# Seven products in the fourth column group of a chunked-attention and feed-forward kernel

## The chip, the cores and the metric

The kernel runs on one core of one Trainium2 chip. The metric is the device time of one execution in microseconds; the kernel before is given by the median of three executions. One further execution was profiled, and every row below comes from that one.

## The reference

The inputs are q, k and v of shape (8, 8, 576, 64) in float32 (batch, heads, sequence, head dimension) and two weight matrices. Attention looks only within chunks of 64 positions:

```python
scores = scale * np.matmul(q_c, k_c.transpose(0, 1, 2, 4, 3))
scores = scores - np.max(scores, axis=-1, keepdims=True)
attn = np.exp(scores)
attn = attn / (np.sum(attn, axis=-1, keepdims=True) + 1e-09)
out = np.matmul(attn, v_c)
...
h = x @ w_in            # x: 4608 x 512, w_in: 512 x 2048
g = h - np.tanh(h)
return g @ w_out        # w_out: 2048 x 512
```

## The kernel before, in words

The 4608 tokens are 36 pairs of 64-token chunks, in nine groups of four pairs (512 tokens). Groups 0 and 1 go through `FeedForward`; groups 2 to 8 go through `Fast`, each as two halves of 256 tokens (b = 0, 1). A half is done in eight **units**, one for each column group j = 0 to 7; column group j is the pair of 128-column blocks j and j + 8 of `w_in`. So a group takes 16 units; unit number s counts from 0 at group 2, and group 4 begins at s = 32. While one group runs, the attention of the next one is prepared between its units.

**A unit** has a first product (x times `w_in`, into the PSUM tile `ph`), the nonlinearity (ScalarE's tanh at line 725, VectorE's `shrink` at line 732, three GpSimd additions at lines 733 to 735), a split into two float16 parts (`gh` on ScalarE, line 744, and `gl` on VectorE, line 745) and a second product (`gemm2`, line 764), which is itself done with seven products. Each float16 product is three terms, high by high, low by high and high by low. The stages of one unit are spread over four units of TensorE's order: in unit s the kernel issues the first product of s, the tanh and shrink of s - 1, the split of s - 2 and the second product of s - 3. `ph` has two buffers.

**The first product has two forms.** In `gemm1` (line 691) it is 24 matmuls of 256 columns. From group 4 on (`SEVEN = 4`, blocked operands) it can also be seven block products (`Fast.seven`, matmuls on line 706), 42 matmuls of 128 columns. These need sums of weight blocks, made once for each j, and sums of x blocks, made once for each half. The seven products come in two parts. Four of them (P5, P4, P1, P6; 24 matmuls) are issued first. Then `kept_back` (ScalarE, line 711) copies three quarters of `ph` to SBUF and `joined` (VectorE, lines 715 and 716) adds two of them up in `ph`. After `gemm2` the other three products (P2, P7, P3; 18 matmuls) accumulate on what `joined` wrote, so they wait for it. One unit later `completed` (VectorE, line 721) does the last additions, ahead of the tanh of that unit. `in_seven` (line 955) decides which units take this form: in the kernel before all from group 4 on, but not j = 3, not j = 0 to 3 of group 4's first half, and not j = 6, 7 of group 8's second half. That is 65 of the 80 units.

**The order of issue** is written out: each engine runs its instructions in program order. `run` (line 812) calls the stages of a unit, and at two places in each unit it calls what stands in the list `at`: `at[o + 2 * s]` after the first product, ahead of tanh, `kept_back` and `joined`; `at[o + 2 * s + 1]` at the unit's end. `beside` (line 958) and `ahead` (line 998) put the attention's steps of group g into those lists by unit and part, the functions of one place in the order of `put`. For the groups from 5 on, in units counted within the running group and alike for both halves (u = 3 and u = 11): `scores` in unit 4 (12), part 1; `largest`, `shifted`, `exponent`, `totals`, `divided`, `high`, `transpose` (two transposing DMAs on SyncE), the split of v, then `values` (96 small matmuls) in part 0 and `blocks` in part 1 of units 11 and 19, that is of j = 3 of either half. `blocks` (line 416) issues, twice, a ScalarE multiply to float16 (line 425), a ScalarE multiply to float32 (line 426) and a VectorE subtraction (line 427). `halves` (line 304, VectorE, line 311) is in part 0 of the unit after, j = 4. `finish` (line 768; five VectorE additions at line 777) follows the second product of j = 7, which is issued in the unit j = 2 of the next half.

`spread` (line 283) puts a broadcast of the greatest |v| by two TensorE matmuls (line 290) into a corner of a PSUM bank of the second product, and `greatest` (line 292, VectorE, line 296) reads it; the second product can't write that bank before. It needs both `halves`. For group 4, `spread` and `greatest` stand in unit 8 of group 3's run.

**The weight-block sums** (`Half.seven`, line 535): a generator of seven steps for each j, six GpSimd operations (lines 539 to 548), two ScalarE copies (lines 560 and 564), two VectorE subtractions (line 556) and, but for j = 7, two DMAs into DRAM (`kept`). `make_in` (line 1243) runs the steps in the lists; before, there are seven such j (none for j = 3), one every 7.25 half-units, beginning 22 half-units before group 3 and ending 28 half-units into it. In the blocked stage the sums of j = 0 to 5 are loaded again from `kept` for each half, two units ahead, into one of three buffers (`load`, line 841).

In the opening, written as the string `PLAN`, a token F*n* issues n matmuls of 512 columns on a zero tile (`warm`, line 1102), which compute nothing that is used.

Of the kernel before, what the change touches and what calls it, by code (L numbers as in the profile page):

```python
# [23 lines left out]
H = 8  # L24
# [7 lines left out]
FC = DFF // P  # L32
# [23 lines left out]
l0.0 A0 A1 l1.0 v0 v1 a2 a3 l0.1 v2 v3 l1.1 l2.0 l2.1 a4 a5 l3.0 l3.1 F15 x0.0 b0.0 i0.0 z0.0 W0.0 S0 S1 q0 x1.0 m0 p0 e1 P1 F13 S2 N0 T0 b1.0 i1.0 S3 N1 x0.1 z1.0 W1.0 T1 F2 m2 p2 e3 U2 V0 F3 G0.0 D2 P3.0 P3.1 b0.1 U3 D3 i0.1 t T2 x1.1 b1.1 G1.0 t T3 s i1.1 z0.1 W0.1 F2 V2 s z1.1 W1.1 H Y G0.1 x2 G1.1 b2 t s i2 t x3 z2.0 w2.0 s z2.1 w2.1 H h S4 S5 b3 i3 | l4.0 l4.1 v4 v5 z3.0 w3.0 z3.1 w3.1 M4 g2 h l5.0 l5.1 c4 M5 g3 h N4 N5 T4 T5 V4 a6 a7 l6.0 l6.1 c5 S6 S7 v6 v7 g4 h E6 l7.0 l7.1 c6 g5 h M7 l8.0 l8.1 c7 g6 h n6 N7 g7 h T6 T7 V6 Z c8 l9.0 l9.1 c9 g8 h l10.0 l10.1 c10 g9 h l11.0 l11.1 c11 g10 h X l12.0 l12.1 c12 g11 h l13.0 l13.1 c13 g12 h l14.0 l14.1 c14 g13 h l15.0 l15.1 c15 g14 h  # L56
# [3 lines left out]
def attn_ffn_kernel(ctx: ExitStack, tc: tile.TileContext, qE, kE, vE, qL, kL, vL, w_in, w_out, out):  # L60
# [894 lines left out]
    def in_seven(g, b, j):  # L955
        return j != 3 and (g, b, j // 4) != (SEVEN, 0, 0) and (g, b, j // 6) != (NG - 1, 1, 1)

    def beside(att, at, g):
# [7 lines left out]
        late = 2 * (g == SEVEN)  # L966
        put(4 + late, 0, att.halves, g, 1)
        put(6 + late, 0, att.spread, g)
        put(6 + late, 1, att.greatest, g)
        put(12, 1, lambda: powers.update({g: half.power_of(g)}))  # L970
        for b, u in enumerate((3, 11)):
# [9 lines left out]
            put(u + 6, 1, att.split_high, g, b)  # L981
            put(u + 7, 0, att.split_low, g, b)
# [8 lines left out]
            if g + 1 < NG:  # L991
                for i in range(2):
                    p = FIRST[g + 1] + 2 * b + i, 2 * b + i
                    put(u + 2 + i, 1, att.load, *p, "q")
                    put(u + 4 + i, 1, att.load, *p, "k")
                    put(u + 7, 1, att.load, *p, "v")

    def ahead(att, at, g):
# [17 lines left out]
        for b, u in enumerate((3, 13) if late else (6, 14)):  # L1016
# [5 lines left out]
            u += late - before * (1 + b)  # L1022
            for i in (2 * b, 2 * b + 1):
                put(u + 2, 1, att.load, FIRST[g + 1] + i, i, "qk")
            put(u + 2, 0, att.scores, g, b)
# [217 lines left out]
    def make_in(i, j):  # L1243
        if j not in made_in:
            made_in[j] = half.seven(j, temporary[i % 2] if i else stream[2], stream[i % 2] if j < FC // 2 - 1 else temporary[1], j == FC // 2 - 1)
# [5 lines left out]
    steps = [[29 * i // 4 - 22 + k for k in (0, 1, 2, 4, 5, 6, 7)] for i in range(FC // 2 - 1)]  # L1251
# [86 lines left out]
```

## Time and profile before

| | |
|---|---|
| median of three executions | 788.44 us (787.76 to 788.88) |
| the profiled execution, its own time | 788.26 us |
| its span, first to last instruction | 786.5 us |
| TensorE busy | 769.9 us, 98% of the span, 9832 matmuls |
| VectorE busy | 635.7 us, 81% |
| ScalarE busy | 480.0 us, 61% |
| GpSimd busy | 501.9 us, 64% |
| mean granted TensorE clock | 0.998 |
| HBM traffic over the span | 105 GB/s |

The profiled execution is 0.18 us below the median; 1.8 us of it lie outside the span. Busy time of TensorE is modelled and overlaps between neighbours, so the share alone doesn't say that TensorE is the bound; the gaps between its instructions do. In the rows PE is TensorE, PEld its weight loads, DVE VectorE, ACT ScalarE, POOL GpSimd and SP SyncE.

### The profile page before, as it was taken

The page shows a single profiled execution, that of the slowest core. Times are in us where ns is not written, and L with a number is a line of the kernel's source. Part 1 is how long each engine was busy: PE and PEld are TensorE (multiplying, and loading weights), DVE is VectorE, ACT ScalarE, POOL GpSimd, SP SyncE. Part 2 cuts the span into 40 slices and gives each one's busy share as a digit, 9 for nine tenths or more (in the row PEclk, how much of TensorE's full clock was granted, in tenths as well). Part 3 has the DMA queues.
Part 4 walks back from the last instruction along what each step waited for, and adds up shares of the span by engine and source line. Part 5 has one row for each costly group of instructions (what it writes and reads, how often), then busy time and mean ns, then how long its engine had stood idle before and what let it go on. Part 6 is the DMA issues. An engine that isn't in the chain of part 4 may idle for free. (4 is left out here: it accounts for less than half of the span.)

```text
span 786.5 us, 23238 instructions
## 1 busy us (share of the span) xinstructions
PE 769.9 (98%) x9832; PEld 663.8 (84%) x9835; DVE 635.7 (81%) x1021; ACT 480.0 (61%) x787; POOL 501.9 (64%) x572
## 2 busy tenths in 40 slices
PE   7999999999999999989999999999999999999997
PEld 4878886666788878878899998999899989999996
DVE  5896998788698888697878887888888878797565
ACT  5877988556466454454656574747565656566443
POOL 1100001587678888789677778677867786868763
PEclk9999999999999999999999999999999999999999
DMA  9865441210232323133262635354544442424110
GB/s 349 289 201 181 162 161 53 78 31 1 82 81 95 82 83 103 49 94 122 65 230 60 202 67 176 96 173 98 156 113 139 127 144 57 135 56 135 55 55 28
DMA packets 74600, 91.68 MB, mean 117 GB/s; under 512 B 34560, under 2 KB 41728, under 8 KB 74496
## 3 DMA queue, kind: packets, MB, share of 16 engines
q1 hardware_dynamic: 74064, 89.55, 36.9%
q8 instruction: 77, 1.26, 0.7%
q10 hardware_dynamic: 432, 0.66, 0.3%
q14 instruction: 27, 0.22, 0.1%
HBM read 70.25 MB, written 12.58 MB: 105 GB/s over the span
## 5 line engine op out<-in xcount | busy, mean ns | idle before, releaser
L733 POOL TENSOR_TENSOR xl<-xl 128x256 f32<-128x256 f32 x111 | 146.5, 1320 | 114.7 <-DVE xl L732 103.2
L725 ACT ACTIVATE t<-ph,sig 128x512 f32<-128x512 f32 x112 | 77.0, 687 | 152.6 <-DVE ph L721 123.2
L691 PE MATMUL ph<-xh,wh 128*128 128x256 f16 x1068 | 123.7, 273 | 0.2 <-DVE xl L732 0.2
L691 PEld LDWEIGHTS <-wh 128*128 128x128 f16 x1068 | 103.5, 98 | 12.9 <-issue 0.9
L732 DVE SCALAR_TENSOR_TENSOR xl<-ph,sig,t 128x512 f32<-128x512 f32 x112 | 83.2, 743 | 28.8 <-ACT t L725 28.6
L706 PE MATMUL ph<-xh,wl 128*128 128x128 f16 x1344 | 97.8, 219 | 0.0
L764 PEld LDWEIGHTS <-gh 128*128 128x128 f16 x924 | 88.1, 98 | 10.1 <-issue 0.4
L706 PE MATMUL ph<-xh,wh 128*128 128x128 f16 x1332 | 95.7, 219 | 0.9 <-DVE ph L716 0.8
L764 PEld LDWEIGHTS <-wl 128*128 128x128 f16 x882 | 85.2, 98 | 12.2 <-issue 2.6
L745 DVE SCALAR_TENSOR_TENSOR gl<-xl,to_g,gh 128x896 f16<-128x896 f32 x68 | 84.8, 1246 | 8.8 <-ACT gh L744 8.8
L764 PE MATMUL po<-wl,gh 128*128 128x256 f16 x610 | 87.9, 273 | 0.2 <-DVE wl L777 0.2
L706 PEld LDWEIGHTS <-wh 128*128 128x128 f16 x1332 | 81.7, 98 | 4.8 <-DVE ph L716 3.6
L764 PE MATMUL po<-wl,wl 128*128 128x256 f16 x549 | 82.1, 273 | 2.5 <-DVE most L296 2.5
L735 POOL TENSOR_TENSOR xl<-xl 128x256 f32<-128x256 f32 x111 | 82.7, 745 | 0.0
L706 PEld LDWEIGHTS <-wl 128*128 128x128 f16 x1344 | 81.0, 98 | 0.8
L744 ACT ACTIVATE gh<-xl,to_g 128x896 f16<-128x896 f32 x68 | 71.0, 1044 | 15.1 <-POOL xl L735 14.8
L734 POOL TENSOR_TENSOR xl<-xl 128x128 f32<-128x128 f32 x111 | 69.4, 625 | 0.0
L745 DVE SCALAR_TENSOR_TENSOR wl<-xl,to_g,wl 128x896 f16<-128x896 f32 x44 | 56.1, 1274 | 4.6 <-ACT wl L744 4.6
L605 PE MATMUL ph<-xh,wh 128*128 128x512 f16 (+2 forms) x252 | 59.7, 380 | 0.0
L764 PE MATMUL po<-wh,wl 128*128 128x256 f16 x333 | 59.7, 273 | 0.0
L744 ACT ACTIVATE wl<-xl,to_g 128x896 f16<-128x896 f32 x44 | 45.9, 1043 | 15.7 <-POOL xl L735 14.6
L636 PE MATMUL po<-wh,gh 128*128 128x512 f32 x128 | 52.8, 415 | 0.0
(231 smaller groups left out, 1599.2 us busy)
## 6 DMA issues: line engine op xcount, KB each, us to landing
wl<-kept SPq DMA_DIRECT2D x96, 256.0 KB, 3.8
raw<-w_in SPq DMA_DIRECT2D x16, 512.0 KB, 3.7
raw<-w_out SPq DMA_DIRECT2D x16, 512.0 KB, 4.8
xl<-qL SPq DMA_DIRECT2D x28, 256.0 KB, 3.9
rawv<-vL SPq DMA_DIRECT2D x28, 256.0 KB, 3.0
rawk<-kL SPq DMA_DIRECT2D x28, 256.0 KB, 4.5
out<-wl SPq DMA_DIRECT2D x55, 128.0 KB, 2.4
kept<-wl SPq DMA_DIRECT2D x12, 256.0 KB, 2.1
```

The lines of the kernel that those rows point to most:

```text
L605: nc.tensor.matmul(ph, lhsT=w[:, kc * P:(kc + 1) * P], rhs=x[b][:, kc, cols], start=(k == 0), stop=(k == 3 * KC - 1))
L636: nc.tensor.matmul(self.po[t], lhsT=gg[a][:, ts], rhs=wt[fc][1][b], start=(fc == 0 and a == b == 0), stop=(fc == FC - 1 and a == 1))
L691: nc.tensor.matmul(self.ph[:, 1 - f::2, :], lhsT=half_w[fc][:, w, kc * P:(kc + 1) * P], rhs=rhs, start=(k == 0), stop=(k == 3 * KC - 1))
L706: nc.tensor.matmul(ph[:, o], lhsT=a[:, w, i * P:(i + 1) * P], rhs=x[v][:, m, i * P:(i + 1) * P], start=(n == "P5" and k == i == 0), stop=( ...
L725: nc.scalar.activation(t, self.ph, AF.Tanh, scale=self.powers[0])
L732: nc.vector.scalar_tensor_tensor(out=u[:, :4], in0=self.ph, scalar=sig, in1=t, op0=ALU.mult, op1=ALU.subtract)
L733: engine.tensor_add(u[:, 4:6], u[:, 1:3], u[:, 0:4:3])
L734: engine.tensor_add(u[:, 6], u[:, 1], u[:, 2])
L735: engine.tensor_sub(u[:, 0:4:3], u[:, 0:2], u[:, 2:4])
L744: nc.scalar.activation(gh, u, AF.Copy, scale=powers[1])
L745: nc.vector.scalar_tensor_tensor(out=gl, in0=u, scalar=powers[1], in1=gh, op0=ALU.mult, op1=ALU.subtract)
L764: nc.tensor.matmul(place[m], lhsT=part[:, self.SUM[m]], rhs=w[m][:, o], start=first, stop=(last and part is gl), skip_group_check=True)
```

## The change

Six things are edited.

1. `in_seven` no longer leaves out j = 3, and of group 4's first half it leaves out only j = 0 and 1. So j = 3 of nine other halves and j = 2, 3 of that one change from 24 matmuls to seven products: eleven units more, 76 of 80. Nothing in the order of a unit's stages changes.
2. The sums of j = 3 are made too: eight generators, one every 6.5 half-units, the first where it was, the last ending three half-units later. The temporary tiles of odd and even ones are exchanged.
3. For group 4, `halves` of the second half, `spread` and `greatest` move: `halves` from unit 6, part 0 to unit 5, part 0; `spread` from unit 8, part 0 and `greatest` from unit 8, part 1 to unit 5, part 1. For the groups after it they keep their places and go last in their lists.
4. The split of v of group 4's first half moves by half a unit: its ScalarE part from unit 9, part 1 to part 0, its VectorE part from unit 10, part 0 to unit 9, part 1.
5. `scores` of group 3's second half moves from part 0 to part 1 of its unit (s = 14), behind the second product; in all groups of `ahead` it is put ahead of the loads of q and k.
6. In `PLAN` one F13 becomes F17.

```diff
-... P1 F13 S2 ...
+... P1 F17 S2 ...
...
     def in_seven(g, b, j):
-        return j != 3 and (g, b, j // 4) != (SEVEN, 0, 0) and (g, b, j // 6) != (NG - 1, 1, 1)
+        return (g, b, j // 2) != (SEVEN, 0, 0) and (g, b, j // 6) != (NG - 1, 1, 1)
...
         put(-4, 0, att.halves, g, 0)
-        late = 2 * (g == SEVEN)
+        late = g == SEVEN
         put(4 + late, 0, att.halves, g, 1)
-        put(6 + late, 0, att.spread, g)
-        put(6 + late, 1, att.greatest, g)
...
-            put(u + 6, 1, att.split_high, g, b)
-            put(u + 7, 0, att.split_low, g, b)
+            put(u + 6, not first, att.split_high, g, b)
+            put(u + 7 - first, first, att.split_low, g, b)
...
+        put(6 - late, late, att.spread, g)
+        put(6 - late, 1, att.greatest, g)
...
+            put(u + 2, before and b, att.scores, g, b)
             for i in (2 * b, 2 * b + 1):
                 put(u + 2, 1, att.load, FIRST[g + 1] + i, i, "qk")
-            put(u + 2, 0, att.scores, g, b)
...
-            made_in[j] = half.seven(j, temporary[i % 2] if i else stream[2], ...)
+            made_in[j] = half.seven(j, temporary[1 - i % 2] if i else stream[2], ...)
...
-    steps = [[29 * i // 4 - 22 + k for k in (0, 1, 2, 4, 5, 6, 7)] for i in range(FC // 2 - 1)]
+    steps = [[(13 * i - 43) // 2 + k for k in (0, 1, 2, 4, 5, 6, 7)] for i in range(FC // 2)]
```

## Rows read from the trace of the kernel before

**Rows 1.** The page's list of engines (busy us, share of the span, instructions).

```profile
PE 769.9 (98%) x9832; PEld 663.8 (84%) x9835; DVE 635.7 (81%) x1021; ACT 480.0 (61%) x787; POOL 501.9 (64%) x572
```

**Rows 2.** Waits of PE from 60 us on: us in total, times, longest.

```profile
PE po L764 <- DVE most L296: 2.5, 1, 2.5
PE psa L351 <- DVE xh L414: 1.9, 1, 1.9
PE ph L706 <- DVE ph L716: 0.8, 3, 0.3
PE psa L351 <- DVE wl L340: 0.6, 1, 0.6
```

**Rows 3.** Timeline of PE, first half of group 6, units j = 3 and 4: start us, us.

```profile
552.46 2.78 PE L691 MATMUL ph<-xh,wh 128*128 128x256 f16 x24
555.17 0.98 PE L351 MATMUL psa<-aT,wl 64*64 64x64 f16 x96
...
558.38 0.50 PE L706 MATMUL ph<-xh,wl 128*128 128x128 f16 x6
...
559.72 0.38 PE L764 MATMUL po<-wh,wl 128*128 128x256 f16 x2
...
562.45 0.51 PE L706 MATMUL ph<-xh,wh 128*128 128x128 f16 x6 [0.27 <-DVE ph L716]
```

**Rows 4.** Timeline of DVE in the same two units.

```profile
554.37 0.42 DVE L721 TENSOR_TENSOR ph<-ph,t 128x256 f32<-128x256 f32 x1
555.54 0.75 DVE L732 SCALAR_TENSOR_TENSOR xl<-ph,sig,t 128x512 f32<-128x512 f32 x1 [0.76 <-ACT t L725]
556.47 1.57 DVE L745 SCALAR_TENSOR_TENSOR wl<-xl,to_g,wl 128x896 f16<-128x896 f32 x1 [0.18 <-ACT wl L744]
557.97 0.68 DVE L427 SCALAR_TENSOR_TENSOR xh<-psa,xh 128x512 f16<-128x512 f32 x1
559.79 0.69 DVE L427 SCALAR_TENSOR_TENSOR xh<-psa,xh 128x512 f16<-128x512 f32 x1 [1.15 <-ACT wh L426]
560.40 1.21 DVE L311 TENSOR_REDUCE v<-rawv 128x1 f32<-128x1024 f32 x1
...
562.10 0.30 DVE L716 TENSOR_TENSOR ph<-ph,t 128x128 f32<-128x128 f32 x1
```

**Rows 5.** Timeline of ACT in the same two units.

```profile
554.82 0.69 ACT L725 ACTIVATE t<-ph,sig 128x512 f32<-128x512 f32 x1 [2.73 <-DVE ph L721]
555.40 1.03 ACT L744 ACTIVATE wl<-xl,to_g 128x896 f16<-128x896 f32 x1
...
559.64 0.69 ACT L725 ACTIVATE t<-ph,sig 128x512 f32<-128x512 f32 x1
560.21 0.49 ACT L711 COPY t<-ph 128x384 f32<-128x384 f32 x1
```

**Rows 6.** Timeline of POOL at 556.4 us.

```profile
556.37 0.72 POOL L733 TENSOR_TENSOR xl<-xl 128x256 f32<-128x256 f32 x1
```

**Rows 7.** Timeline of DVE, then of PE, group 3's run, unit 5 (s = 21).

```profile
320.60 1.15 DVE L745 SCALAR_TENSOR_TENSOR gl<-xl,to_g,gh 128x896 f16<-128x896 f32 x1 [0.25 <-ACT gh L744]
...
322.06 2.79 PE L691 MATMUL ph<-xh,wh 128*128 128x256 f16 x24
```

**Rows 8.** Groups of DVE between 340 and 400 us: busy us, mean ns.

```profile
L556 DVE TENSOR_TENSOR wh<-wh,wh 128x512 f16<-128x512 f32 x2 | 2.5, 1242 | 0.0
```

**Rows 9.** Groups of POOL between 344 and 372 us.

```profile
L545 POOL TENSOR_TENSOR wh<-wh,wh 128x256 f32<-128x256 f32 x2 | 2.2, 1090 | 0.2
```

**Rows 10.** Windows: us, then busy us of PE, PEld, DVE, ACT, POOL; PEclk, DMA share, GB/s.

```profile
18.00:25.00 7.00, 6.44 (x47) 5.49 (x47) 4.83 (x12) 5.59 (x23) 0.00 (x0) 0.76 0.83 285
...
346.00:377.00 31.00, 30.24 (x417) 26.74 (x415) 25.64 (x32) 16.85 (x25) 30.22 (x34) 1.00 0.34 101
```

**Rows 11.** Timeline of PE, the opening's second fill.

```profile
8.28 2.75 PE L1102 MATMUL ph<-warm 128*128 128x512 bf16 x12 [0.16 <-issue]
11.42 0.69 PE L186 MATMUL psa<-k,q 64*64 64x64 f32 x32 [0.38 <-DMA k<-kE]
```

**Rows 12.** The page's DMA issues: KB each, median us to landing.

```profile
wl<-kept SPq DMA_DIRECT2D x96, 256.0 KB, 3.8
```

More of the change, by code (lines that the diff above doesn't have):

```diff
@@ L55 @@
 PLAN = """
-l0.0 A0 A1 l1.0 v0 v1 a2 a3 l0.1 v2 v3 l1.1 l2.0 l2.1 a4 a5 l3.0 l3.1 F15 x0.0 b0.0 i0.0 z0.0 W0.0 S0 S1 q0 x1.0 m0 p0 e1 P1 F13 S2 N0 T0 b1.0 i1.0 S3 N1 x0.1 z1.0 W1.0 T1 F2 m2 p2 e3 U2 V0 F3 G0.0 D2 P3.0 P3.1 b0.1 U3 D3 i0.1 t T2 x1.1 b1.1 G1.0 t T3 s i1.1 z0.1 W0.1 F2 V2 s z1.1 W1.1 H Y G0.1 x2 G1.1 b2 t s i2 t x3 z2.0 w2.0 s z2.1 w2.1 H h S4 S5 b3 i3 | l4.0 l4.1 v4 v5 z3.0 w3.0 z3.1 w3.1 M4 g2 h l5.0 l5.1 c4 M5 g3 h N4 N5 T4 T5 V4 a6 a7 l6.0 l6.1 c5 S6 S7 v6 v7 g4 h E6 l7.0 l7.1 c6 g5 h M7 l8.0 l8.1 c7 g6 h n6 N7 g7 h T6 T7 V6 Z c8 l9.0 l9.1 c9 g8 h l10.0 l10.1 c10 g9 h l11.0 l11.1 c11 g10 h X l12.0 l12.1 c12 g11 h l13.0 l13.1 c13 g12 h l14.0 l14.1 c14 g13 h l15.0 l15.1 c15 g14 h
+l0.0 A0 A1 l1.0 v0 v1 a2 a3 l0.1 v2 v3 l1.1 l2.0 l2.1 a4 a5 l3.0 l3.1 F15 x0.0 b0.0 i0.0 z0.0 W0.0 S0 S1 q0 x1.0 m0 p0 e1 P1 F17 S2 N0 T0 b1.0 i1.0 S3 N1 x0.1 z1.0 W1.0 T1 F2 m2 p2 e3 U2 V0 F3 G0.0 D2 P3.0 P3.1 b0.1 U3 D3 i0.1 t T2 x1.1 b1.1 G1.0 t T3 s i1.1 z0.1 W0.1 F2 V2 s z1.1 W1.1 H Y G0.1 x2 G1.1 b2 t s i2 t x3 z2.0 w2.0 s z2.1 w2.1 H h S4 S5 b3 i3 | l4.0 l4.1 v4 v5 z3.0 w3.0 z3.1 w3.1 M4 g2 h l5.0 l5.1 c4 M5 g3 h N4 N5 T4 T5 V4 a6 a7 l6.0 l6.1 c5 S6 S7 v6 v7 g4 h E6 l7.0 l7.1 c6 g5 h M7 l8.0 l8.1 c7 g6 h n6 N7 g7 h T6 T7 V6 Z c8 l9.0 l9.1 c9 g8 h l10.0 l10.1 c10 g9 h l11.0 l11.1 c11 g10 h X l12.0 l12.1 c12 g11 h l13.0 l13.1 c13 g12 h l14.0 l14.1 c14 g13 h l15.0 l15.1 c15 g14 h
 """
@@ L1244, in make_in @@
         if j not in made_in:
-            made_in[j] = half.seven(j, temporary[i % 2] if i else stream[2], stream[i % 2] if j < FC // 2 - 1 else temporary[1], j == FC // 2 - 1)
+            made_in[j] = half.seven(j, temporary[1 - i % 2] if i else stream[2], stream[i % 2] if j < FC // 2 - 1 else temporary[1], j == FC // 2 - 1)
         next(made_in[j])
```

## The prediction

> **What bounds the kernel now.** I read the page's list of engines first: TensorE is busy for 98% of the span [rows 1]. As that share is modelled, I then asked who waits for whom on TensorE. From 60 us on, the waits that end at another engine are few: 2.5 us once for `greatest`, 1.9 us once for the release of a PSUM tile by the attention's result, 0.6 us once for the split of v, and three of up to 0.3 us for `joined` [rows 2]. So TensorE works without a gap nearly everywhere, and a matmul saved is time saved, as long as the other engines are ready earlier too. The view that decides whether they are is the timeline of one half around j = 3, engine by engine [rows 3 to 5]. The reader should see there that the unit j = 4 already waits: P2 starts at 562.45 after 0.27 us idle, released by `joined`, whose second addition ends at 562.40. VectorE is late there by nothing to spare, and j = 3 is the unit just before it.
>
> **What a unit saves.** In [rows 3] the plain unit holds TensorE from 552.46 to 555.17, 2.71 us. The first 24 small matmuls of the next unit take from 558.38 to 559.72, 1.34 us, so 42 at that pace take 2.35 us. A unit saves 0.36 us, and eleven save 4.0 us if nobody makes TensorE wait.
>
> **What a half pays at j = 4.** `blocks` runs in j = 3, and everything that seven products add to j = 3 goes into the same two in-order queues. I walk the half of [rows 3 to 5] again with the added instructions. `completed` of j = 2 ends at 554.79 and tanh at 555.51 as before. Now ScalarE issues `kept_back` (0.49, and 0.57 from a tanh's start to its own in [rows 5]): 555.39 to 555.88. VectorE, idle for 0.76 us there before, must issue `joined` ahead of `shrink`: two additions of 0.30 [rows 4], one after the other, some 0.63 us, end 556.54. `shrink` (0.75) ends at about 557.2; `gh` (1.03) is done by 556.9, so `gl` starts at about 557.1 instead of 556.47. With 1.15 us [rows 7] it ends at 558.25. The first subtraction of `blocks` starts at 558.15 (before: 557.97), and the second 1.82 us later, as in [rows 4], since ScalarE's second pair stands between: 559.97. Then `completed` of j = 3, which is new, takes 0.42 and ends at 561.0. In the old trace 2.61 us pass from the second subtraction's start to the end of `joined` (559.79 to 562.40), with `halves` (1.21) in it; with `completed` added and 0.18 of start, `joined` ends at 562.40 + 0.18 + 0.4 = 562.95. ScalarE is no later: tanh of j = 3, which must now wait for `completed`, runs to 561.7 and `kept_back` to 562.2.
>
> TensorE comes 0.36 us earlier: to 562.18 - 0.36 = 561.82. It waits 1.1 us instead of 0.27, and P2 starts about 0.53 us later than before. The saving of j = 3 is gone and some more. That j = 3 itself waits I don't expect: its `joined` ends at 556.54, and TensorE gets to its P2 at 552.46 + 1.34 + 3.21 (small matmuls, `values` and second product, 555.17 to 558.38) = 557.0.
>
> Nine halves have `blocks` in j = 3. The list counts three waits [rows 2], so the other halves just meet or have a little to spare. For seven halves I take +0.53 each, 3.7 us. In the first half of group 4 (where j = 0 to 3 were plain) and of group 8 (nothing to reduce for a group 9) there was no wait: 1.1 - 0.36 = 0.75 each, 1.5 us. The last half has no `blocks` and saves 0.3. Together **+4.9 us**. The row that this leans on most is `gl`. At its old place it took 1.57 us, starting 0.10 us after POOL's addition [rows 4, 6]; where it started first it took 1.15 [rows 7]. In the new order `shrink` releases that addition some 0.2 us after `gl` begins, so I take 1.15; with 1.57 a half pays 0.4 more, 3.8 us over nine, the upper end. The lower end is no lateness at all from the queues, -0.36 a half. What the rows show fits the Trainium skill (SBUF — State Buffer, section Who interferes with whom): the pair of ports that VectorE and GpSimd share is locked for a whole instruction by whoever issues first, and issue order decides who blocks. By that rule alone the price hangs on a start that differs by 0.1 us: about +0.5 a half when VectorE is first, about +0.95 when GpSimd is.
>
> **What the moved steps give.** `scores` of group 3's second half waited 1.9 us [rows 2]; now the second product of that unit stands in front, which is longer than the wait, so I take the whole, **-1.9** (bounds -1.9 and 0, if the next release is late instead). The steps behind `scores` on VectorE need it at the same time as before, and the q and k loads behind it on SyncE start no later.
>
> `spread` and `greatest` of group 4 move from unit 8, where VectorE was late by 2.5 us [rows 2], to unit 5. There `gl` ends at 321.75, `halves` would end at 321.75 + 1.21 = 322.96, and TensorE is free for `spread` at 322.06, when the next first product began [rows 7]. So a wait of some 1.2 us with the short additions replaces one of 2.5: **-1.3** (bounds -2.5 and 0). The earlier split of v takes away the 0.6 us wait: **-0.5** (0 to -0.6).
>
> **What the eighth set of sums costs.** Two VectorE subtractions of 1.24 [rows 8], two ScalarE copies and six GpSimd operations (four like the 1.09 of [rows 9], two of twice the elements: at most 8.7 us). They lie beside TensorE, which needs none of them for two units. But the last set now ends three half-units later, so that a subtraction of 1.24 comes into group 4's opening units between `totals` and `divided`. I take **+0.6**, half of it; bounds 0 and the 8.7 us of GpSimd. The loads of the sums become 22 more on SyncE; each landed after 3.8 us [rows 12], against two units of lead (a unit of seven products and its second product, 4.6 us). They cost nothing, and if that cover went, up to 3.8 us once for each.
>
> **The longer fill.** Twelve recorded matmuls of F13 take from 8.28 to about 11.0, and the next scores start at 11.42, when a load lands [rows 11]. Four more at 2.75 / 12 = 0.23 us end at about 11.9: 0.5 us later at that point, in a stretch where TensorE is idle half of the time afterwards. I take **+0.2** (0 to +0.9). The mean granted clock between 18 and 25 us is 0.76 [rows 10]: TensorE dropped to its 1.2 GHz level there, after a stretch with idle gaps. The Trainium skill (TensorE: Matmul & The Clock Gate, What's actually happening) says that idleness throttles and activity releases. By that rule more filling might take the drop away. The row prices it [rows 10]: (1 - 0.76) x 7 us = 1.7 us at the most. I don't count it, as the fill lies seven microseconds ahead of the drop.
>
> **The sum.** 4.9 - 1.9 - 1.3 - 0.5 + 0.6 + 0.2 = +2.0 us. The profiled execution took 788.26, so I forecast 790.3. That is 1.9 us over the median of 788.44, which is 0.18 above the profiled execution. A measurement of this kernel can tell 0.2%, 1.6 us, from no change; the forecast is just beyond.
>
> **The rivals.**
> - *The saving holds.* Place: `joined` of j = 4. If the chain through `blocks` finishes when TensorE comes, as it does now in most halves, each of nine halves saves 0.36 and the old waits stay. Then -0.36 x 11 = -4.0, with -1.9 - 1.3 - 0.5 + 0.8: -6.9, 781.4. It decides where a half's lateness falls under 0.2 us: the other terms give -2.9 - 0.3 + 9 x 0.18 = -1.6. For it speaks that VectorE is only 81% busy [rows 1]; against it, that the wait is on an order, not on a share, and that j = 4 already waits.
> - *The moved waits come back.* If VectorE, ScalarE and GpSimd are what limits group 3's run, TensorE comes earlier and waits for them at the next unit. Then the 3.7 us are not gained: 4.9 + 0.8 = +5.7, 794.0. For it speaks that GpSimd is busy for 30.22 of 31 us there [rows 10].
> - *GpSimd becomes the bound there.* A set more, denser than before, in a stretch with 0.8 us to spare: 8.7 - 0.8 = 7.9 at most, half of it likely: +4, on top of the forecast, 794.3.
> - *`gl` loses the port.* +3.8, 794.1.
> - *The clock drop goes.* -1.7: 788.6.
> - *The change saves less than its matmuls:* if 42 small ones in these units keep the pace of 24 large ones, nothing is saved, +0.36 on the last half only. The 65 units that have them speak against it; it would move the sum by under 0.5.
>
> **How the numbers follow.** The forecast, 0.38, with its own range of 788 to 793; the saving holds, 0.18; the waits come back, 0.15; GpSimd, 0.08; the port, 0.11; the clock, 0.10. The range of 785.0 to 795.5 leaves out most of the first rival and the tails of GpSimd. Faster by over 0.2% (under 786.9): the first rival, and what lies below in the forecast and the clock, 0.25. Slower (over 790.0): more than half of the forecast and the three slow rivals, 0.53. Within: 0.22.
>
> **What would show it.** In the changed profile: a wait of TensorE for `joined` (line 716) in nearly every half, about 1.1 us at j = 4, ten times instead of three; the idle 0.76 us of VectorE before `shrink` filled; a wait for line 296 of about 1 us or a wait before line 290 in group 3's run; no wait for line 414. The period between the halves' j = 4 should grow by about 0.5 us. I am wrong if that wait stays under 0.5 us, or if new waits on `shrink` stand in group 3's run.

## The result, and the profile after

The changed kernel takes 798.07 us, the median of four runs (797.36 to 798.55). The kernel before, in four runs beside it, takes 788.66. The ratio is 1.0116, with a 95% interval of 1.0101 to 1.0131: slower by 9.4 us. The direction was forecast; the size, +2.0, was not, and 798.07 lies above the range. The profiled execution took 798.48 with a span of 796.5, 10.0 over the span of before. Executions of one kernel go with their mean granted clock: of the 48 of before that ran beside the experiments, the 29 at 0.999 or 1.000 took 786.9 to 788.3 us, and the 19 at 0.996 to 0.998 took 787.9 to 790.2.

The page's list of engines after, whose columns are those of [rows 1]:

```profile
PE 770.4 (97%) x10037; PEld 664.6 (83%) x10037; DVE 643.7 (81%) x1056; ACT 485.7 (61%) x800; POOL 509.7 (64%) x578
```

TensorE's busy time stands where it stood, with 205 instructions more, while the span grew by 10 us: those 10 us are gaps, or work that went slower. The waits of PE from 60 us on say which gaps (us in total, times, longest), and answer to [rows 2]:

```profile
PE ph L706 <- DVE ph L716: 10.0, 10, 1.5
PE po L290 <- DVE sums L313: 2.8, 1, 2.8
PE ph L706 <- DVE xl L732: 1.8, 1, 1.8
PE psa L351 <- issue: 1.6, 2, 1.0
PE po L764 <- DVE wl L777: 0.9, 2, 0.7
```

The reader should see three things. The wait for `joined` (line 716) has grown from 0.8 us in three to 10.0 in ten. The three waits of [rows 2] that the moved steps were to remove (lines 296, 414, 340) are gone. In their place stand waits that were not there: one of 2.8 for the sums of `spread`, one of 1.8 for `shrink`, and smaller ones ahead of the scores and for the finish.

**One half, unit by unit.** The timelines of the first half of group 6, units j = 3 and 4, answer to [rows 3 to 6]. Times of before and after stand 6.34 us apart here (`completed` of j = 2 ends at 554.79 and at 561.13). First PE; the last row is P2 of j = 4:

```profile
563.45 0.50 PE L706 MATMUL ph<-xh,wh 128*128 128x128 f16 x6
...
567.98 0.27 PE L764 MATMUL po<-wl,wl 128*128 128x256 f16 x1
569.34 0.51 PE L706 MATMUL ph<-xh,wh 128*128 128x128 f16 x6 [1.09 <-DVE ph L716]
```

Then DVE, and under it POOL, in the same stretch:

```profile
562.59 0.30 DVE L716 TENSOR_TENSOR ph<-ph,t 128x128 f32<-128x128 f32 x1
562.80 0.74 DVE L732 SCALAR_TENSOR_TENSOR xl<-ph,sig,t 128x512 f32<-128x512 f32 x1
563.45 1.14 DVE L745 SCALAR_TENSOR_TENSOR wl<-xl,to_g,wl 128x896 f16<-128x896 f32 x1
564.51 0.68 DVE L427 SCALAR_TENSOR_TENSOR xh<-psa,xh 128x512 f16<-128x512 f32 x1
566.35 0.69 DVE L427 SCALAR_TENSOR_TENSOR xh<-psa,xh 128x512 f16<-128x512 f32 x1 [1.15 <-ACT wh L426]
566.96 0.42 DVE L721 TENSOR_TENSOR ph<-ph,t 128x256 f32<-128x256 f32 x1
567.29 1.21 DVE L311 TENSOR_REDUCE v<-rawv 128x1 f32<-128x1024 f32 x1
...
568.99 0.30 DVE L716 TENSOR_TENSOR ph<-ph,t 128x128 f32<-128x128 f32 x1
```

```profile
563.62 1.56 POOL L733 TENSOR_TENSOR xl<-xl 128x256 f32<-128x256 f32 x1 [1.05 <-DVE xl L732]
```

Read from the top, this is the walk of the prediction: `joined` of j = 3, `shrink`, the split's second part at 1.14, two subtractions of `blocks` 1.84 apart, the new `completed` at 566.96, `halves`, and only then `joined` of j = 4, which ends at 569.29. TensorE had its last matmul before it at 567.98 and waits 1.09 us.

**Group 3's run, where `spread` now stands.** PE, then DVE, around unit 5:

```profile
319.54 1.16 PE L351 MATMUL psa<-rawk,xl 64*64 64x64 f32 x64 [0.54 <-issue]
323.50 0.80 PE L290 MATMUL po<-ident,sums 128*128 128x128 f32 x2 [2.80 <-DVE sums L313]
324.09 5.20 PE L691 MATMUL ph<-xh,wh 128*128 128x256 f16 x24
```

```profile
320.93 1.14 DVE L745 SCALAR_TENSOR_TENSOR gl<-xl,to_g,gh 128x896 f16<-128x896 f32 x1
321.99 1.21 DVE L311 TENSOR_REDUCE v<-rawv 128x1 f32<-128x1024 f32 x1
323.23 0.21 DVE L313 TENSOR_SCALAR sums<-v 128x1 f32<-128x1 f32 x1
```

`spread` (line 290) stands right behind the scores, with no product between. TensorE is free for it at 320.70 and gets its sums at 323.44. The 24 matmuls behind it take 5.20 us where the same 24 took 2.79 [rows 7]. The windows show why (columns as in [rows 10]; PEclk is the third number from the end):

```profile
318.00:322.00 4.00, 2.16 (x74) 1.71 (x71) 3.85 (x6) 2.36 (x4) 3.77 (x6) 1.00 0.20 69
322.00:329.00 7.00, 5.50 (x25) 4.03 (x26) 2.79 (x8) 0.00 (x0) 2.85 (x4) 0.51 0.44 145
```

In the wait, after a stretch in which TensorE did little and then nothing, its granted clock falls to the lower of its two levels (1.2 GHz): it is 1.00 over 320.7 to 322.2 us and 0.50 over 322.2 to 323.5, and 0.51 over 322 to 329. The rule of the Trainium skill (TensorE: Matmul & The Clock Gate, What's actually happening), that idleness throttles and activity releases, agrees with it: 0.51 here, against 1.00 in the runs below where the wait is gone; the last section has waits after which the clock stayed up.

**Where the 10 us came from.** I laid the start of each unit's product after beside the one before and took the steps in the difference of the two timelines:

| stretch | after minus before | forecast |
| --- | --- | --- |
| opening | -1.2 | +0.2 |
| scores of group 3's second half | -1.8 | -1.9 |
| `spread` and `greatest`: wait 2.8, half clock 2.4, the wait before the scores 0.5, the wait for line 296 -2.5, and 0.4 as the two matmuls of `spread` take 0.59 (323.50 to 324.09) in place of 0.23 (334.51 to 334.74) | +3.6 | -1.3 |
| the split of v | -0.7 | -0.5 |
| waits for the finish (0.9), before scores (0.8) and for `shrink` (1.6) at 309, 363 and 390 us | +3.4 | +0.6 |
| the halves of groups 4 to 8 | +6.9 | +4.9 |
| sum | +10.2 | +2.0 |

The sum is taken at the last second product; the span ends 10.0 later.

### The profile page after: what moved, and what is told of

It reads as the page before. It is cut to its first block, busy times and chain, and to the rows that moved or that the text cites. A ratio compares the mean times of both kernels' runs of the same rounds, so it can differ in the third digit from the quotient of the medians.

```text
span 796.5 us, 23769 instructions
## 1 busy us (share of the span) xinstructions
PE 770.4 (97%) x10037; PEld 664.6 (83%) x10037; DVE 643.7 (81%) x1056; ACT 485.7 (61%) x800; POOL 509.7 (64%) x578
## 4 chain that ended last, share of the span: by engine, by line
PE 56%; DVE 23%; POOL 9%; ACT 6%; issue 5%; DMA 1%; POOLq 0%; DVEq 0%; SPq 0%; ACTq 0%
PE ph L706 17%; PE po L764 14%; PE po L636 10%; PE ph L605 9%; DVE gl L745 3%; DVE xl L732 2%; PE ph L691 2%; POOL xl L733 2%; DVE wl L745 2%; ACT t L711 2%; DVE wl L777 1%; PE psa L351 1%; POOL xl L735 1%; PE psa L186 1%; POOL xl L734 1%
## 5 line engine op out<-in xcount | busy, mean ns | idle before, releaser
L733 POOL TENSOR_TENSOR xl<-xl 128x256 f32<-128x256 f32 x111 | 155.9, 1405 | 124.0 <-DVE xl L732 113.2
L706 PE MATMUL ph<-xh,wh 128*128 128x128 f16 x1530 | 110.4, 219 | 10.0 <-DVE ph L716 10.0
L706 PE MATMUL ph<-xh,wl 128*128 128x128 f16 x1608 | 114.7, 219 | 1.8 <-DVE xl L732 1.8
L706 PEld LDWEIGHTS <-wh 128*128 128x128 f16 x1530 | 93.8, 98 | 15.2 <-DVE ph L716 13.8
L706 PEld LDWEIGHTS <-wl 128*128 128x128 f16 x1608 | 95.9, 98 | 2.6 <-issue 2.0
L691 PE MATMUL ph<-xh,wh 128*128 128x256 f16 x804 | 95.5, 277 | 0.0
L764 PEld LDWEIGHTS <-wl 128*128 128x128 f16 x882 | 85.2, 98 | 9.6
L691 PEld LDWEIGHTS <-wh 128*128 128x128 f16 x804 | 79.3, 99 | 10.9 <-issue 0.5
L745 DVE SCALAR_TENSOR_TENSOR gl<-xl,to_g,gh 128x896 f16<-128x896 f32 x68 | 82.1, 1208 | 7.6 <-ACT gh L744 7.6
L735 POOL TENSOR_TENSOR xl<-xl 128x256 f32<-128x256 f32 x111 | 82.9, 746 | 0.0
L715 DVE TENSOR_TENSOR ph<-ph,t 128x128 f32<-128x128 f32 x76 | 22.7, 298 | 47.3 <-ACT t L711 46.4
L734 POOL TENSOR_TENSOR xl<-xl 128x128 f32<-128x128 f32 x111 | 59.6, 537 | 0.0
L745 DVE SCALAR_TENSOR_TENSOR wl<-xl,to_g,wl 128x896 f16<-128x896 f32 x44 | 53.6, 1219 | 4.7 <-ACT wl L744 4.6
```

What stands on the lines that cost most here:

```text
L691: nc.tensor.matmul(self.ph[:, 1 - f::2, :], lhsT=half_w[fc][:, w, kc * P:(kc + 1) * P], rhs=rhs, start=(k == 0), stop=(k == 3 * KC - 1))
L706: nc.tensor.matmul(ph[:, o], lhsT=a[:, w, i * P:(i + 1) * P], rhs=x[v][:, m, i * P:(i + 1) * P], start=(n == "P5" and k == i == 0), stop=( ...
L733: engine.tensor_add(u[:, 4:6], u[:, 1:3], u[:, 0:4:3])
L734: engine.tensor_add(u[:, 6], u[:, 1], u[:, 2])
L735: engine.tensor_sub(u[:, 0:4:3], u[:, 0:2], u[:, 2:4])
L745: nc.vector.scalar_tensor_tensor(out=gl, in0=u, scalar=powers[1], in1=gh, op0=ALU.mult, op1=ALU.subtract)
```

## The experiments

Each diff is against the kernel after, where nothing else is said. The runs of before differ a little between chips (medians of 787.79 to 788.66), so each ratio is to the runs of before on its own chip, and a difference of two medians from two chips is given with the one by the ratios.

### Without j = 3

```diff
-        return (g, b, j // 2) != (SEVEN, 0, 0) and (g, b, j // 6) != (NG - 1, 1, 1)
+        return j != 3 and (g, b, j // 2) != (SEVEN, 0, 0) and (g, b, j // 6) != (NG - 1, 1, 1)
...
-    wanted = [j for j in range(FC // 2) if any(in_seven(g, b, j) for g in range(SEVEN, NG) for b in range(2))]
+    wanted = list(range(FC // 2))
```

> The changed kernel with j = 3 plain again in all halves (its block sums are still made, and everything else of the change stays). Theory: the nine waits of about 1.0 us for the second addition of joined at j = 4 come from the stages that seven products add to j = 3. Then they fall back to at most 0.3 us, the halves from the second of group 4 on have their old period, and the time falls by about 6.5 us, to 791.5. Rival: the halves are longer because of the 22 further loads and the denser traffic of SyncE while the waits only show where it ends; as the loads of j = 3 go too here, that rival expects the same time, and only the run with another order tells them apart. Second rival: the loss is made in group 3's run, not in the halves; then the time stays within 1 us of 798.1.

Measured: 790.91 us (789.5 to 792.2), ratio 1.0034 [1.0021, 1.0047]. Two of its waits of PE:

```profile
PE ph L706 <- DVE ph L716: 1.5, 4, 0.6
PE po L290 <- DVE sums L313: 2.8, 1, 2.8
```

The waits for `joined` are back to the few of [rows 2], all eight sets being made still. 7.2 us are gone by the medians, 6.5 by the ratios; in the two profiles the halves give back 6.3, and 1.0 is a shorter stretch at the lower clock behind `spread` (the 24 matmuls take 4.45 there, not 5.20). So j = 3's products cost most of what the halves lost in the table, 6.9; the remaining 2.7 to 3.1 over before lie in group 3's run and at the start of group 4.

### The order inside unit j = 4

`kept_back` (one ScalarE instruction) and `joined` (two of VectorE) go ahead of the `completed` and tanh of the unit before.

```diff
+                first = unit["seven"] and unit["j"] == 4
+                if first:
+                    self.kept_back(unit)
+                    self.joined(unit)
                 if pending:
                     closing(pending)
...
-                if unit["seven"]:
+                if unit["seven"] and not first:
                     self.kept_back(unit)
                     self.joined(unit)
```

> The changed kernel, but in the units j = 4 that use seven products, kept_back and joined are issued ahead of the additions that complete j = 3, of its tanh and of halves. No instruction is added or taken away. Theory (a matter of order in VectorE's and ScalarE's queues): the wait for joined at j = 4, nine times about 1.0 us, shrinks to under 0.2 us, and the time falls by 8 to 9.5 us, to 788.5 to 790. Rival (VectorE and ScalarE have no time left in these units, or the loads are what is late): the wait appears in another place, for the shrink of j = 3 or for the release of the attention's PSUM tile, and the time stays within 2 us of 798.1.

Measured: 791.63 (789.09 to 793.12), ratio 1.0036 [1.0021, 1.0052]. Its row of the same wait:

```profile
PE ph L706 <- DVE ph L716: 3.2, 5, 0.8
```

No matmul was removed, and 6.5 us are gone (6.3 by the ratios); the waits at j = 4 with them. The 22 further loads are all there too, so they weren't the cause. So the loss was one of order: `joined` stood behind 0.42 us of `completed` and 1.21 of `halves` that nobody needed yet. It fell short of the forecast since four waits of 0.6 to 0.8 appear at j = 5 of every other half, behind the six short VectorE steps of `power_of` (lines 578 to 583), and one of 0.3 in the last half: the lateness was handed on.

### `spread` and `greatest` at their old place

```diff
-        late = g == SEVEN
+        late = 2 * (g == SEVEN)
...
-            put(u + 6, not first, att.split_high, g, b)
-            put(u + 7 - first, first, att.split_low, g, b)
+            put(u + 6, 1, att.split_high, g, b)
+            put(u + 7, 0, att.split_low, g, b)
...
-        put(6 - late, late, att.spread, g)
-        put(6 - late, 1, att.greatest, g)
+        put(6 + late, 0, att.spread, g)
+        put(6 + late, 1, att.greatest, g)
```

> The changed kernel with halves, spread, greatest and the split of group 4 back at their old places. Theory (the new place of spread costs): the wait of 2.8 us ahead of line 290 goes, and with it the 6.8 us at the half clock from 322 us on, which cost 2.4 us; a wait of 2.5 us or more for line 296 and one of 0.6 us for line 340 come back. Together 2 to 3 us less, 795 to 796. Rival (the eighth set of sums makes group 3's run late whatever the places): the half clock stays or a longer wait for line 296 takes its place, and the time stays within 1 us of 798.1.

Measured: 794.32 (794.05 to 794.38), ratio 1.0065 [1.0046, 1.0084], 3.8 us under the kernel after (4.0 by the ratios), a little more than expected. Its two waits that matter, and the window that answers to the one above:

```profile
PE po L764 <- DVE most L296: 1.9, 1, 1.9
PE psa L351 <- DVE wl L340: 0.4, 1, 0.4
```

```profile
322.00:329.00 7.00, 7.00 (x67) 6.29 (x65) 5.61 (x7) 1.73 (x2) 7.00 (x8) 1.00 0.46 152
```

The old waits come back, 2.3 us, and yet it is faster. In the two profiles TensorE is 5.9 us earlier behind unit 5, of which the clock is 2.4, and 1.1 more at 360 us, where the wait of 1.0 ahead of group 4's second scores (`issue` in the kernel after) is gone too; 2.9 go back at the old places.

### One product between the scores and `spread`

`spread` at unit 6, part 0, `greatest` in part 1:

```diff
-        put(6 - late, late, att.spread, g)
-        put(6 - late, 1, att.greatest, g)
+        put(6, 0, att.spread, g)
+        put(6, 1, att.greatest, g)
```

> The changed kernel with group 4's spread half a unit later, behind the next first product (unit 6, part 0), and greatest in part 1 of that unit; halves stays at its new place. Theory (spread waits for halves only because it stands right behind the scores, and the clock's fall follows from that wait): the wait of 2.8 us ahead of line 290 goes, the granted clock stays at 2.4 GHz from 322 us on, and at most 1 us of wait for line 296 comes in their place. The part in the wait that is not given back later is 3 to 5 us: 793 to 795. Rival (TensorE runs ahead there and waits at the next place in any case): the wait for line 296 or for the shrink grows by as much, and the time stays within 1 us of the changed kernel's 797.3 to 798.1.

Measured: 792.1 (792.0 to 792.5), ratio 1.0051 [1.0036, 1.0066]: 6.0 under the kernel after (5.1 by the ratios), and more than expected. Neither the wait for line 290 nor the one for line 296 stands among its waits of PE, of the two ahead of scores the one of 1.0 is gone here too, and the clock stays up:

```profile
PE psa L351 <- issue: 0.5, 1, 0.5
```

```profile
322.00:329.00 7.00, 6.93 (x63) 5.99 (x62) 6.75 (x9) 1.77 (x3) 7.00 (x8) 1.00 0.52 156
```

A move by half a unit too far had turned a gain into the loss of 3.6 in the table, and into the 0.8 at 363 us as well. Half a unit later, the unit's first product of 2.8 us covers the sums.

### The fill of 13

```diff
-e1 P1 F17 S2
+e1 P1 F13 S2
```

> The changed kernel with F13 in place of F17. In the profiles the changed kernel is ahead by 1.2 us when group 1's feed-forward begins its second half, and the half clock between 18 and 22 us, seen before, is not there. Theory (the longer fill keeps the clock up): without it the half clock comes back near 18 us and the time rises by 1.2 us, to 799.3. Rival (where the clock's drop falls has nothing to do with these four matmuls): the time stays within 0.5 us, and the drop is there in one run and not in another.

Measured: 797.29 (797.19 to 801.53), ratio 1.0117 [1.0085, 1.0148]: no difference from the kernel after. Its window in the opening:

```profile
18.00:25.00 7.00, 6.35 (x101) 5.03 (x99) 5.76 (x13) 6.30 (x25) 0.30 (x1) 1.00 0.89 294
```

The clock drop of [rows 10] isn't there with the short fill either, so the fill had not removed it; nor is it there in the two runs below that start from the kernel before, with its 13 matmuls. The -1.2 of the opening belongs to the execution that was profiled and not to the change.

### The seven products and the set alone

The kernel **before**, with the wider `in_seven` and the eighth set at the old spacing (the two buffers exchanged, as in the change):

```diff
-        return j != 3 and (g, b, j // 4) != (SEVEN, 0, 0) and (g, b, j // 6) != (NG - 1, 1, 1)
+        return (g, b, j // 2) != (SEVEN, 0, 0) and (g, b, j // 6) != (NG - 1, 1, 1)
...
-    steps = [[29 * i // 4 - 22 + k for k in (0, 1, 2, 4, 5, 6, 7)] for i in range(FC // 2 - 1)]
+    steps = [[29 * i // 4 - 22 + k for k in (0, 1, 2, 4, 5, 6, 7)] for i in range(FC // 2)]
```

> The kernel before with the two things that the eleven units need, and no more: in_seven and an eighth set of block sums at the old spacing of 7.25 half-units (the last one ends three and a half half-units later than in the changed kernel). The moves of scores, spread, halves and the split, the denser spacing and F17 are left out. Theory: the nine waits at j = 4 cost 6 to 7 us whatever group 3's run does, the waits of 1.9 us ahead of the scores and 2.5 us for line 296 are there as before, and the last set costs 1 to 2 us at the start of group 4: 788 + 6.5 + 1.5 = 796. Rival (the moves and the density are what costs): the time stays under 793.

Measured: 797.47 (797.17 to 798.66), ratio 1.0121 [1.0106, 1.0136]. Its four largest waits of PE:

```profile
PE ph L706 <- DVE ph L716: 7.8, 9, 1.1
PE ph L706 <- DVE xl L732: 3.0, 1, 3.0
PE po L764 <- DVE most L296: 2.5, 1, 2.5
PE psa L351 <- DVE xh L414: 2.1, 1, 2.1
```

The eleven units and their set cost 9.2 us without any of the moves. The moves, the denser spacing and the fill together leave the time where it is. In the table the scores and the split gain 2.5 and `spread` costs 3.6; against that, this run pays more at the start of group 4, where the wait for `shrink` is 3.0 in place of 1.8 and the granted clock behind it is 0.57 (389 to 393 us).

### The scores alone

The kernel **before** with the scores of a second half issued in the unit's second part:

```diff
+            put(u + 2, before and b, att.scores, g, b)
             for i in (2 * b, 2 * b + 1):
                 put(u + 2, 1, att.load, FIRST[g + 1] + i, i, "qk")
-            put(u + 2, 0, att.scores, g, b)
```

> The kernel before with nothing but the scores of group 3's second half moved behind the second product. Theory: the wait of 1.9 us ahead of these scores goes, and no other grows, since the engines behind it had time: 1.5 to 1.9 us less than the kernel before, 786.3 to 786.7. Rival (TensorE, coming 1.8 us earlier, waits for the additions of finish and ahead of group 4's first scores, as the changed kernel does with 0.7 and 0.5 us, and later for line 296): at most 0.6 us are left, 787.6 to 788.2.

Measured: 786.37 (785.12 to 787.93), ratio 0.9978 [0.9968, 0.9988]: 1.85 us faster, as the term said (-1.9). The wait for line 414 is gone from its list, the one for line 296 is not:

```profile
PE po L764 <- DVE most L296: 2.5, 1, 2.5
```

### The repairs together

The order of j = 4 and the later `spread`, and `power_of` a unit later, away from j = 5:

```diff
-        put(12, 1, lambda: powers.update({g: half.power_of(g)}))
+        put(13, 1, lambda: powers.update({g: half.power_of(g)}))
```

> The changed kernel with kept_back and joined of j = 4 ahead of the completion of j = 3, with group 4's spread behind the next first product, and with the six small VectorE steps that make a group's scales (lines 578 to 583) one unit later, as they stand ahead of joined of j = 5, for which four waits of 0.6 to 0.8 us were left. Theory: the waits in the halves fall under 0.3 us, and the parts add: 797.5 - 6.5 - 3 - 3 = 785, 2 to 3 us under the kernel before. Rival (what the halves and group 3's run give is the same slack of VectorE): the parts don't add, the waits for the shrink at the start of group 4 grow, and the time stays at 788 or above.

Measured: 785.17 (784.76 to 785.4), ratio 0.9961 [0.9946, 0.9976], below the kernel before.

```profile
PE ph L706 <- DVE ph L716: 2.3, 8, 0.4
PE ph L706 <- DVE xl L732: 2.2, 2, 1.9
```

The ten waits for `joined` have become eight of at most 0.4, and the largest left is the one for `shrink`, at the end of the set's making.

### The last set later

The same with steps of the last two sets moved: the later ones of the seventh half a unit earlier, the last one of the eighth two units later:

```diff
+    steps[6], steps[7] = [17 + k for k in range(7)], [24, 25, 26, 28, 29, 30, 35]
```

> As e7_combined, and the VectorE subtractions of the last two sets of block sums are moved: those of the seventh set one half-unit earlier, the last one of the eighth set two units later, so that none stands between totals and divided of group 4's second half or ahead of blocks of its first. Theory (each subtraction of 1.2 us stood in a chain that TensorE waits for): the wait of 1.9 us for the shrink at the start of group 4 and the 1.0 us ahead of group 4's second scores shrink by about 1 us each, 1 to 2 us less than e7_combined. Rival (GpSimd, not VectorE, sets when those are ready): the same time as e7_combined within 0.5 us.

Measured: 785.1 (784.96 to 785.34), ratio 0.9962 [0.9948, 0.9976]: no gain. The wait for `shrink` is 1.5 in place of 1.9. What leads to it, on POOL and then ACT:

```profile
374.75 0.73 POOL L547 TENSOR_TENSOR wh<-wh,wh 128x256 f32<-128x256 f32 x1
375.56 0.73 POOL L548 TENSOR_TENSOR wh<-wh 128x256 f32<-128x256 f32 x1
376.24 2.00 POOL L442 TENSOR_TENSOR xh<-wl,xh 128x512 f16<-128x512 f32 x1
...
379.30 0.74 POOL L735 TENSOR_TENSOR xl<-xl 128x256 f32<-128x256 f32 x1
```

```profile
380.07 1.04 ACT L744 ACTIVATE wl<-xl,to_g 128x896 f16<-128x896 f32 x1 [3.14 <-POOL xl L735]
```

VectorE no longer has a subtraction of a set between `totals` and `divided`, but ScalarE's split waits 3.14 us for GpSimd, which works without a gap through the set's additions (lines 547 and 548) and the attention's differences (line 442). So the set's price isn't VectorE's 1.24 alone: with that out of the way, GpSimd is late, as the rival said.

### The repairs without j = 3

The repaired kernel, all eight sets made, with:

```diff
-        return (g, b, j // 2) != (SEVEN, 0, 0) and (g, b, j // 6) != (NG - 1, 1, 1)
+        return j != 3 and (g, b, j // 2) != (SEVEN, 0, 0) and (g, b, j // 6) != (NG - 1, 1, 1)
```

> e7_combined with j = 3 plain again in all halves (its sums are still made). Theory: with the new order the ten units save TensorE what their matmuls say, 0.3 us each, less the small waits that are left (0.25 us twice in a group): 785.2 + 2 to 3 = 787 to 788. Rival (the order alone and the moves of group 3's run give the whole gain, and the seven products at j = 3 still cost): the time falls below 785.

Measured: 784.95 (784.6 to 785.12), ratio 0.9958 [0.9943, 0.9973]: the same as with j = 3's products, 785.17 (it meets the rival's "below 785" by no more than the spread of its runs). The theory that the repaired order lets them gain 2 to 3 us falls. The timelines of both runs say where the gain goes. Take the first half of group 6. From P2 of j = 2 to P2 of j = 4 it is 548.22 to 558.78 here, 10.56 us, and 547.70 to 558.28 with j = 3's products, 10.58. There the work is shorter by 0.28, and a stall of 0.30 between P2 of j = 3 and the first products of j = 4, which the trace puts down to no engine, takes it back. With j = 3's products, the same 18 matmuls behind P2 of j = 2 and of j = 3:

```profile
548.03 1.17 PE L706 MATMUL ph<-xh,wl 128*128 128x128 f16 x18
553.68 1.47 PE L706 MATMUL ph<-xh,wl 128*128 128x128 f16 x18
```

The second half of group 6 loses it to another such stall, 0.33 inside a second product at 592.47 (`issue`). The other halves lose it elsewhere, or keep it. The first halves of groups 5 and 7 keep 0.27 us. The second halves of groups 4, 5 and 7 end within 0.08 of where they would be without, as a wait of 0.25 to 0.42 for `joined` of j = 4 comes in. The two halves of group 8 lose 0.46 and 0.56, with waits of 0.37 for `shrink` and 0.32 for `joined`. Up to the end of group 7 the products gain 0.7 us in all, and group 8 gives back 1.0.

### Without the eighth set

The run above without the set that nobody reads then, at the spacing of 6.5 (and the buffers as before):

```diff
-            made_in[j] = half.seven(j, temporary[1 - i % 2] if i else stream[2], stream[i % 2] if j < FC // 2 - 1 else temporary[1], j == FC // 2 - 1)
+            made_in[j] = half.seven(j, temporary[i % 2] if i else stream[2], stream[i % 2] if j < FC // 2 - 1 else temporary[1], j == FC // 2 - 1)
...
-    wanted = list(range(FC // 2))
+    wanted = [j for j in range(FC // 2) if any(in_seven(g, b, j) for g in range(SEVEN, NG) for b in range(2))]
```

> e10_combined_no_j3 without the eighth set of block sums (that of j = 3, which nothing uses there), at the changed kernel's spacing of 6.5 half-units. Theory (the eighth set, which ends three half-units later, makes the shrink late at the start of group 4): the wait of 1.9 us for line 732 there falls under 0.5 us and the time falls by about 1.5 us, to 783.4. Rival (TensorE comes 3 us earlier by the moves and would wait there for its other engines in any case): the wait stays over 1.2 us and the time within 0.6 us of 785.0.

Measured: 782.95 (782.83 to 783.15), ratio 0.9933 [0.9916, 0.995], the fastest of all. Its waits of PE:

```profile
PE ph L706 <- DVE ph L716: 1.0, 4, 0.3
PE po L764 <- DVE wl L777: 0.9, 2, 0.7
```

The wait for `shrink` is gone with the set, and 2.0 us with it. Of the change it keeps the scores, the early split of v, the denser spacing, the fill and the seven products for j = 2 of group 4's first half, with `spread` at unit 6; and it has the new order of j = 4 and the later `power_of`.

### The same at the old spacing

```diff
-    steps = [[(13 * i - 43) // 2 + k for k in (0, 1, 2, 4, 5, 6, 7)] for i in range(FC // 2)]
+    steps = [[29 * i // 4 - 22 + k for k in (0, 1, 2, 4, 5, 6, 7)] for i in range(FC // 2)]
```

> As e12_seven_sets, at the old spacing of 7.25 half-units. If the denser spacing is what makes TensorE wait for finish (0.7 us) and ahead of group 4's first scores (0.55 us), both go and the time falls by up to 1.2 us more, to 782.2; if those waits come from TensorE's earlier arrival, they stay and the time is that of e12_seven_sets within 0.6 us.

Measured: 783.8 (783.66 to 785.46), ratio 0.9949 [0.9933, 0.9965]. Neither expectation of the time was right: the median is 0.85 above that of the denser one, the two intervals overlapping.

```profile
PE ph L706 <- DVE xl L732: 1.5, 1, 1.5
PE psa L351 <- DVE xh L427: 1.3, 1, 1.3
PE po L764 <- DVE wl L777: 0.2, 1, 0.2
```

The wider spacing takes the waits at the finish (0.7 to 0.2) and before group 4's first scores (0.5) away, so it is the denser one that makes those. But two others come, 2.8 us together, ahead of group 4's second scores and for `shrink`. In the kernel before, with the same seven sets at the same spacing, these two places waited 0.2 each, and TensorE came there some 6 us later: that reads as the rival of the moved waits, though no run takes the cause apart.

## Why the prediction was right in its direction and wrong in its size

**What a half pays (forecast +4.9, found +6.9): the mechanism was right.** With the 6.34 us taken off, `joined` of j = 3 ends at 556.55 (forecast 556.54), the split's second part at 558.25 (558.25), the subtractions start at 558.17 and 560.01 (558.15 and 559.97), `completed` ends at 561.04 (561.0), and `joined` of j = 4 at 562.95 (562.95). TensorE waits 1.09 (1.1). The run without j = 3 and the run with the other order agree: 6.5 and 6.3 us come back by the ratios, the latter with every matmul in place.

The terms of the sum were mis-sized. The step "A unit saves 0.36 us" took the plain product's 2.71 us where `values` follow it; where the second product follows, the same 24 take 2.62 start to start (382.18 to 384.80 in the trace of before). The 0.09 between them stays with the small matmuls, and the work ahead of P2 of j = 4 was shorter by 0.28. And "For seven halves I take +0.53 each" carried the half with an old wait of 0.27 over to all. Three of the seven had waited 0.27 to 0.28, three 0.03, and one not at all. With waits of 1.0 to 1.1 after, the loss is 1.09 - 0.27 - 0.28 = 0.54 in the first kind and 1.00 - 0.03 - 0.28 = 0.69 in the second; the timelines show steps of 0.54 to 0.55, of 0.70 to 0.72, and 0.95 in the last. The first halves of groups 4 and 8, taken at 0.75 each, paid 1.35 (the first waited 1.46 where 1.1 was taken) and 0.91. The last half, taken at -0.3, paid 0.2: with no `values` in front, its j = 3 itself waits 0.32 for `joined`. The eleventh unit, j = 2 of group 4's first half, has no term in the sum; it saved 0.27.

**The price of the split's second part was rightly chosen.** It took 1.14, not 1.57. In [rows 4, 6] GpSimd's addition had started 0.10 ahead and took 0.72 while VectorE took 1.57; after, VectorE starts 0.17 ahead, takes 1.14, and the addition takes 1.56. What was argued from the Trainium skill (SBUF — State Buffer, Who interferes with whom), that whoever issues first holds the shared ports, agrees with both pairs of rows in who is held up; VectorE lost 0.43 and GpSimd 0.84, each 0.1 to 0.2 less than what was left of the other's instruction (0.62 and 0.97).

**The scores (-1.9, found -1.8) and the split of v (-0.5, found -0.7)** came as forecast; the scores alone measured -1.85.

**`spread` (-1.3, found +3.6) is the step that failed.** The prediction said: "TensorE is free for `spread` at 322.06, when the next first product began". That was the old kernel's time. The change's own gains bring TensorE there earlier, and in unit 5's second part `spread` stands right behind the scores, with no product ahead: TensorE was free at 320.70. VectorE ended its second split at 322.07, not 321.75; a subtraction of a set (line 556, 0.99 us at 319.36) stands ahead of it now. The wait was 323.50 - 320.70 = 2.8 in place of 1.2. And I gave the idle time no price beyond its length: the clock fell behind it and the next 24 matmuls took 5.20 instead of 2.79. The wait of 1.0 at 363 us, 0.8 in the table's next row, belongs to the place of `spread` too. With one product between, in the run with `spread` at unit 6, both are gone, and so is the old 2.5. So the move was a good one by half a unit less. This is also the rival of the waits that come back, with a price that its text lacked, the clock.

**The eighth set (+0.6, found +3.4 in its row) was mis-sized.** The prediction priced one VectorE subtraction at half its time. Its place was right, as DVE of the kernel after shows:

```profile
385.42 1.22 DVE L556 TENSOR_TENSOR wh<-wh,wh 128x512 f16<-128x512 f32 x1
386.56 1.22 DVE L383 TENSOR_TENSOR psa<-psa,sm 128x1024 f32<-128x1024 f32 x1
...
390.00 0.74 DVE L732 SCALAR_TENSOR_TENSOR xl<-ph,sig,t 128x512 f32<-128x512 f32 x1
```

VectorE has no gap from there to `shrink`. But the split in between, at 387.70, also needs ScalarE's, which ends at 387.17, since it waits for GpSimd:

```profile
386.13 1.04 ACT L744 ACTIVATE wl<-xl,to_g 128x896 f16<-128x896 f32 x1 [3.14 <-POOL xl L735]
```

So the subtraction itself holds `shrink` up by about 0.5 us, an estimate from these rows (387.70 - 387.17); with it out of the way, in the run with the last set later, the wait was 0.4 shorter. With its GpSimd additions the set is worth 2.0 us, at one spacing, as taking it out showed. GpSimd as the bound, the rival at +4, named the engine that the sum had left out, and put its price too high. The wait for the finish isn't the set's: the denser spacing makes it, at 0.7 against 0.2, and with it the 0.5 ahead of group 4's first scores. The sum has no term for the spacing.

**The fill (+0.2)** did nothing, and the rival of the clock in the opening falls with the run at 13.

**That the saving holds,** the fast rival, is false in the strong sense: with the waits at j = 4 taken away, the run without j = 3's products is as fast as the one with them. Small waits at other places take back what ten units saved, 0.28 each; what made the stalls of 0.3 in group 6 stays open.

## What to carry to other kernels

A shorter unit was worth nothing here, as its successor waits on an in-order queue. Walk the queue of the unit behind before counting the matmuls, and look whether the late instruction stands behind work that nobody needs yet. Issuing `kept_back` and `joined` ahead of it gained 6.3 us by the ratios, with every matmul in place. When several steps move at once, the arrival times of one must be worked out with the others' gains in, since the engine now comes earlier; and a step with a wait wants a product ahead of it.

## What the runs showed of the hardware

I had not expected a single wait to cost TensorE its clock in the middle of the kernel. In all four profiles with `spread` right behind the scores, the granted clock falls in that wait or just behind it, to 0.51 over 322 to 329 us in the kernel after and to 0.76 in the others. The 24 matmuls behind it take 5.20, 4.45, 4.39 and 3.99 in place of 2.79, a loss of up to 2.4 us on top of the 2.8. The mean clocks of all executions agree: it is 0.994 to 0.999 in the 28 with `spread` at this place, and 0.999 or 1.000 in 29 of the 30 of the changed kernel and its repairs with `spread` elsewhere. But a wait doesn't bring the lower level each time. In the kernel before, a wait of 2.46 us for line 296 ends at 343.59 and the clock stays at 1.00 (338 to 346 us; 23 recorded matmuls behind it take 2.67 us). In the run with the scores alone the same wait, 2.47 us, is followed by the lower level:

```profile
342.00:346.00 4.00, 4.00 (x24) 2.93 (x23) 3.57 (x4) 3.75 (x5) 3.52 (x5) 0.57 0.35 66
```

There the 24 matmuls took 4.45 us. In the run with the seven products and the set alone, that wait of 2.46 leaves the clock at 1.00 (342 to 346 us), and the one of 3.0 for `shrink` is followed by 0.57 (389 to 393 us). What decides wasn't tried. In the opening the same holds: the drop of [rows 10] is in one of the profiles of this case, without any edit that would explain it.
